# Linear attention with a GELU feed-forward: weights in another row order, and the masks of batch 1 on GpSimd

## The chip, the cores and the metric

One core of one Trainium2 chip. The metric is device time in microseconds (us) of one execution, median over several. The page of a profile covers a slightly shorter span (292.0 us for an execution that took 293.77 us). A "look" is one profiled execution, and there is one per kernel.

## The reference

For 8 batches, 8 heads, 576 tokens and 64 dimensions per head, linear attention and then a feed-forward layer:

```python
def phi(x):
    return np.where(x > 0, x, np.exp(x) - 1.0) + 1.0
q_p, k_p = phi(q), phi(k)
kv = np.einsum('bhsd,bhse->bhde', k_p, v)          # per head 64 x 64
z = np.sum(k_p, axis=2)
num = np.einsum('bhsd,bhde->bhse', q_p, kv)
den = np.einsum('bhsd,bhd->bhs', q_p, z)[..., None] + 1e-06
x = num / den                                       # tokens x 512 after the heads are joined
h = x @ w_in                                        # 512 -> 2048
g = gelu_tanh(h)
out = g @ w_out                                     # 2048 -> 512
```

## The kernel before

TensorE does everything in bf16. Each batch is one stage `j` of the feed-forward layer, with a first half (16 blocks `m` of 128 hidden units, `h_ps`) and a second half (16 slots of four 128x512 matmuls, `o_ps`). The attention of the next batch is placed by hand into slots of these halves. The first 512 tokens of a batch ("main") and the last 64 ("rests") are loaded and handled apart.

The parts that the change touches:

```python
w_in_r = moe_w_in.rearrange("(c p) f -> p c f", p=P)
w_out_r = moe_w_out.rearrange("(i p m) f -> i p m f", p=P, m=4)   # 8-KB runs: 4 rows per partition
# ...
def cast_w_in_halves(i):              # f32 -> bf16 on GpSimd, every fourth column
    for u in range(2):
        nc.gpsimd.tensor_copy(
            out=w_in_sb[:, :, 512 * i + 256 * u : 512 * i + 256 * (u + 1)]
                .rearrange("p c (m x) -> p c m x", m=2),
            in_=w_st[i].rearrange("p c (x m) -> p c m x", m=4)[:, :, 2 * u : 2 * u + 2],
        )

def mask_vrh(b, pairs):               # v's rests times 0 or 1 per partition: keep one pair of heads
    for i in pairs:
        nc.scalar.activation(vrh[b][:, :, i, 0:D], rest_by_head("vr", b), AF.Copy,
                             scale=pair[:, i : i + 1])
# ...
def plan_second():                    # batch 1, inside stage 0
    def exps():                       # ScalarE, after the GELU of block 11
        # ... exp of q (two halves), of k, of k's rests, then the GELU table again
    def phis():                       # VectorE: max(x+1, 1), then the minimum with exp
        for s in halves:
            phi_line(phi["q", b], ld["q", b], s)
            phi_min(phi["q", b], box["q"], s)
        phi["k", b] = phi_of(ld["k", b], box["k"], "k_p")
        phi_krh(1)                    # the rests of k
        mask_vrh(1, range(NP))
    # ...
    at(1, 0, 11, exps)
    at(2, 0, 0, phis)
    at(2, 0, 0, cast_vs)
    for fn, c, slot in (
        (tq, 0, 8), (tq, 1, 8),                  # q transposed, into 2 PSUM buffers
        (lambda c: kv_rests(), 0, 9),            # rests' matmuls, on krh and vrh
        (lambda c: kv(), 0, 10),                 # main sum of k*v
        (lambda c: last_w_out(), 0, 10),
        (nab, 0, 11), (nab, 1, 12),              # q times kv
        # ...
    ):
        at(2, 0, slot, lambda fn=fn, c=c: fn(c))
```

PSUM is the memory into which TensorE writes its results. The two PSUM buffers that `tq`, `kv_rests`, `kv` and `nab` share in turn are also those of blocks 12 to 15 of stage 0, which ScalarE's GELUs have to empty first. Each engine works in program order. GpSimd has, in this order, eight casts of `w_in`, six of `w_out` and a seventh; ScalarE does the eighth.

Of the kernel before, what the change touches and what calls it, by code (L numbers as in the profile page):

```python
# [10 lines left out]
AF = mybir.ActivationFunctionType  # L11
ALU = mybir.AluOpType
# [3 lines left out]
def kernel(  # L16
# [12 lines left out]
    nc = tc.nc  # L29

    B, H, S, D = q.shape
    d_model, d_ff = moe_w_in.shape
    P = 128
# [21 lines left out]
    small = ctx.enter_context(tc.tile_pool(name="small", bufs=1))  # L55

    w_in_r = moe_w_in.rearrange("(c p) f -> p c f", p=P)
    w_out_r = moe_w_out.rearrange("(i p m) f -> i p m f", p=P, m=4)

    w_in_sb = const.tile([P, KM, d_ff], BF16, name="w_in_sb")  # L60
    w_out_sb = const.tile([P, MM, d_model], BF16, name="w_out_sb")
# [15 lines left out]
    def load_rest_half(src, t, m, s, eng):  # L77
        eng.dma_start(
            out=t[REST * s : REST * (s + 1)],
            in_=src[2 * m + s, :, MAIN:S, :].rearrange("h p d -> p h d"),  # L80
        )
# [7 lines left out]
    def load_w_in(i, t=None, f=slice(0, 512)):  # L89
        if t is None:  # L90
            t = pld.tile([P, KM, 512], FP32, name="w_st", tag="ld")
        nc.sync.dma_start(
            out=t[:, :, f], in_=w_in_r[:, :, 512 * i + f.start : 512 * i + f.stop]
        )
        return t

    def load_w_out(i):
        t = pld.tile([P, 4, 512], FP32, name="w_st", tag="ld")
        nc.sync.dma_start(out=t, in_=w_out_r[i])
        return t  # L100

    ld = {}
# [7 lines left out]
    def load_rests(m, names):  # L110
        for n, src in names:
            ld[n, m] = load_rest(src, m, n[0] + "_r", nc.gpsimd)
# [16 lines left out]
    def rest_by_head(n, b):  # L129
        return ld[n, 0][:, C * b : C * b + C]  # L130
# [5 lines left out]
    w_st = [load_w_in(i) for i in range(3)]  # L136
# [14 lines left out]
    pair = small.tile([P, NP], FP32, name="pair")  # L151
# [10 lines left out]
    vrh, krh = [], []  # L162
# [13 lines left out]
    for b in range(2):  # L176
        nc.gpsimd.tensor_copy(
            out=vrh[b][:, :, :, D], in_=pair[:, None, :].to_broadcast([P, C, NP])
# [10 lines left out]
    def gelu_table():  # L189
        nc.scalar.preload_act_table_set("gelu_apprx_tanh_and_others")  # L190

    def cast_w_in_halves(i):
        for u in range(2):

            nc.gpsimd.tensor_copy(  # L195
                out=w_in_sb[
                    :, :, 512 * i + 256 * u : 512 * i + 256 * (u + 1)
                ].rearrange("p c (m x) -> p c m x", m=2),
                in_=w_st[i].rearrange("p c (x m) -> p c m x", m=4)[
                    :, :, 2 * u : 2 * u + 2  # L200
                ],
            )

    def cast_w_out_halves(i, fns):
        for u, fn in enumerate(fns):
            fn(
                out=w_out_sb[:, 4 * i + 2 * u : 4 * i + 2 * u + 2, :],
                in_=wo_st[i][:, 2 * u : 2 * u + 2, :],
            )


    phi = {}
# [4 lines left out]
    def exp_into(e, x, hs=slice(0, H)):  # L217
        nc.scalar.activation(  # L218
            e[:, :, hs, :].rearrange("p c h d -> p h c d"), by_chunk(x[:, hs]), AF.Exp
        )  # L220

    def exp_main(name, b):
        e = pe.tile([P, C, H, D], BF16, name=name + "_e")
        exp_into(e, ld[name, b])
        return e


    def phi_line(xp, x, hs=slice(0, H)):
        nc.vector.tensor_scalar(  # L229
            xp[:, :, hs, :].rearrange("p c h d -> p h c d"), by_chunk(x[:, hs]),  # L230
            1.0, 1.0, op0=ALU.add, op1=ALU.max,
        )

    def phi_min(xp, e, hs=slice(0, H)):
        nc.vector.tensor_tensor(  # L235
            xp[:, :, hs, :], xp[:, :, hs, :], e[:, :, hs, :], op=ALU.min
        )

    def phi_of(x, e, name):
        xp = pphi.tile([P, x.shape[2] // D, H, D], BF16, name=name)  # L240
        phi_line(xp, x)
        phi_min(xp, e)
        return xp
# [7 lines left out]
    def cast_v(b, fn, s=slice(0, H)):  # L251
        fn(
            out=vps[b % 2][:, s, :, 0:D],
            in_=ld["v", b][:, s].rearrange("p h (c d) -> p h c d", d=D),
        )
# [5 lines left out]

    def mask_vrh(b, pairs):
        for i in pairs:
            nc.scalar.activation(
                vrh[b][:, :, i, 0:D], rest_by_head("vr", b), AF.Copy,
                scale=pair[:, i : i + 1],
            )

    def exp_krh(b):
        nc.scalar.activation(krh[b][0][:, :, 0], rest_by_head("kr", b), AF.Exp)  # L270

    def phi_krh(b):

        e, line, kr = krh[b]
        nc.vector.tensor_scalar(
            line[:, :, 0], rest_by_head("kr", b), 1.0, 1.0, op0=ALU.add, op1=ALU.max
        )
        nc.vector.tensor_tensor(line[:, :, 0], line[:, :, 0], e[:, :, 0], op=ALU.min)
        for t in range(2):
            nc.vector.tensor_scalar(  # L280
                kr[:, :, t], line[:, :, 0], odd[:, t : t + 1], None, op0=ALU.mult
            )
# [52 lines left out]
    def t_q(src_of, qt, c0, n, t_ps):  # L335
        for c in range(n):
            for i in range(NP):
                nc.tensor.transpose(  # L338
                    t_ps[:, c, i, :], src_of(c0 + c, i), ident
                )  # L340
# [197 lines left out]
    def at(ph, j, slot, fn):  # L538
        fill.setdefault((ph, j, slot), []).append(fn)
# [92 lines left out]
    def plan_second():  # L632

        b = 1
        box = {}

        def exps():
            box["q"] = pe.tile([P, C, H, D], BF16, name="q_e")
            for s in halves:
                exp_into(box["q"], ld["q", b], s)  # L640
            box["k"] = exp_main("k", b)
            exp_krh(1)
            gelu_table()

        def phis():
            phi["q", b] = pphi.tile([P, C, H, D], BF16, name="q_p")
            for s in halves:
                phi_line(phi["q", b], ld["q", b], s)
                phi_min(phi["q", b], box["q"], s)
            phi["k", b] = phi_of(ld["k", b], box["k"], "k_p")  # L650
            phi_krh(1)
            mask_vrh(1, range(NP))

        def cast_vs():
            cast_v(b, nc.vector.tensor_copy)

        def last_w_out():
            cast_w_out_halves(3, (nc.gpsimd.tensor_copy, nc.scalar.copy))
            load_rests(1, (("kr", k), ("vr", v)))
            for s in range(2):  # L660
                load_rest_half(q, ld["qr", 0], 0, s, nc.gpsimd)
            load_rests(1, (("qr", q),))

        def kv():
            kv_ps = ps_a.tile([P, 2, 512], FP32, name="kv_ps", tag="a")
            for i in range(NP):
                kv_mm(b, i, kv_ps)
            kv_evac(b, kv_ps, second=box["rests"])

        def kv_rests():  # L670
            r_ps = ps_a.tile([P, 2, 512], FP32, name="r_ps", tag="a")
            for a in range(2):
                kv_mm_rests(b, a, r_ps[:, a, 0 : 2 * E])
            box["rests"] = pout.tile([P, 2, d_model], FP32, name="o_sb")[
                :, :, 0 : 2 * E
            ].rearrange("p a (t u) -> p a t u", u=E)
            nc.scalar.copy(
                box["rests"],
                r_ps[:, :, 0 : 2 * E].rearrange("p a (t u) -> p a t u", u=E),
            )  # L680

        def tq(h):
            if h == 0:
                box["qt"] = pt.tile([P, C, NP, P], BF16, name="qt")
            t_ps = ps_a.tile([P, 4, NP, P], BF16, name="t_ps", tag="a")
            t_q(q_src(b), None, 2 * h, 2, t_ps)
            nc.scalar.copy(out=box["qt"][:, 2 * h : 2 * h + 2], in_=t_ps[:, 0:2])

        def nab(c):
            n_ps = ps_a.tile([P, 2, 512], FP32, name="n_ps", tag="a")  # L690
            nab_mm(box["qt"][:, c], kvbds[b], n_ps)
            box["x", c] = nab_evac(n_ps)

        def tx(c):
            copy = nc.scalar.copy if c < 2 else nc.vector.tensor_copy
            pe_tx(b, c, box["x", c], c < 2, copy)

        def early(m):
            first_mm_early(1, m)

        at(1, 0, 11, exps)
        at(2, 0, 0, phis)
        at(2, 0, 0, cast_vs)
        for fn, c, slot in (
            (tq, 0, 8), (tq, 1, 8), (lambda c: kv_rests(), 0, 9), (lambda c: kv(), 0, 10), (lambda c: last_w_out(), 0, 10),
            (nab, 0, 11), (nab, 1, 12), (nab, 2, 13), (tx, 0, 13), (nab, 3, 14),
            (tx, 1, 14), (tx, 2, 15), (early, 0, 15), (early, 1, 15), (tx, 3, 15),
            (early, 2, 15),
        ):
            at(2, 0, slot, lambda fn=fn, c=c: fn(c))  # L710
# [209 lines left out]
```

## Time and profile before

| | before |
|---|---|
| time, median | 293.55 us (293.38 to 293.57) |
| span of the profile | 292.0 us |
| TensorE busy | 283.3 us, 97% |
| second half of stage 0 begins | 33.64 us |
| first product of q with batch 1's sum (`n_ps`) | 46.65 us |

The last two rows are the marks by which kernels are compared: from the first `n_ps` on, TensorE is fed without a gap that the change touches, so a shift there is a shift of the end. Here is, from the timeline of TensorE, the stretch in which batch 1's attention starts (start, duration of the group, instruction, shapes, number; in brackets idle time before and what ended it):

```profile
41.41 1.06 PE L338 MATMUL t_ps<-ident,q_p 128*128 128x128 bf16 x16
...
43.17 0.62 PE L287 MATMUL r_ps<-g 128*128 128x130 bf16 x8
...
44.49 1.10 PE L301 MATMUL kv_ps<-vp,k_p 128*128 128x130 bf16 x16
...
46.65 0.41 PE L344 MATMUL n_ps<-kvbd,qt 128*128 128x130 bf16 x4 [0.20 <-DVE kvbd L328]
```

Transposes, rests, sum and product run without a wait but the last 0.20 us. In the trace the mask tiles bear the name `g`, since they lie in the buffer of a later `g`.

### The profile page before, as it was taken

What the parts mean: (1) busy time and instruction counts of PE and PEld (TensorE: products, weight loads), DVE (VectorE), ACT (ScalarE), POOL (GpSimd) and SP (SyncE); (2) the same over time, 40 slices, a digit from 0 to 9 for tenths busy, and PEclk for the clock granted to TensorE, in tenths of its full rate; (3) what the DMA queues carried; (4) which work ended last, traced back from release to release, by engine and by line L of the source; (5) the groups of instructions that cost most, each with busy time, mean ns of one, the idle gap of its engine ahead of it and who ended that gap; (6) DMA issues with size and microseconds to landing.
All of it is one profiled execution on the core that took longest, in us unless ns stands there. A gap on an engine that the chain in (4) does not pass through costs nothing.

```text
span 292.0 us, 4298 instructions
## 1 busy us (share of the span) xinstructions
PE 283.3 (97%) x1710; PEld 147.6 (51%) x1710; DVE 115.7 (40%) x191; ACT 161.2 (55%) x228; POOL 45.8 (16%) x57
## 2 busy tenths in 40 slices
PE   8789999999999999999999999999999999999994
PEld 7665455645565445544454445444544444444443
DVE  4950495606683692347035642452240000000011
ACT  4847894589955753666356925672551166026400
POOL 7089968300007000000000000000000000000000
PEclk9999999999999999999999999999999999999999
DMA  7999999993379994999922993305140110020032
GB/s 249 378 409 410 362 399 361 325 382 93 72 246 220 287 242 144 290 257 292 332 53 65 288 277 110 72 2 162 54 74 18 72 74 0 31 94 21 0 72 72
DMA packets 62835, 53.75 MB, mean 184 GB/s; under 512 B 31840, under 2 KB 57184, under 8 KB 62304
## 3 DMA queue, kind: packets, MB, share of 16 engines
q1 hardware_dynamic: 59392, 42.35, 51.7%
q10 hardware_dynamic: 2464, 8.52, 7.3%
q0 software_dynamic: 960, 2.62, 3.2%
q8 instruction: 13, 0.21, 0.3%
q14 instruction: 6, 0.05, 0.1%
HBM read 36.70 MB, written 9.44 MB: 158 GB/s over the span
## 4 chain that ended last, share of the span: by engine, by line
PE 87%; POOL 6%; DMA 3%; SPq 1%; DVE 1%; issue 0%; DVEq 0%
PE o_ps L843 41%; PE h_ps L392 39%; POOL w_in_sb L195 6%; DMA w_st<-in_moe_w_in_dram 3%; PE n_ps L344 3%; PE kv_ps L301 2%; PE o_ps L812 1%; SPq L69 1%; PE kv_ps L312 0%; SPq L124 0%; PE t_ps L367 0%; PE t_ps L338 0%; DVE kvbd L328 0%; PE r_ps L287 0%; DVE xt L488 0%
## 5 line engine op out<-in xcount | busy, mean ns | idle before, releaser
L843 PE MATMUL o_ps<-w_out_sb,g 128*128 128x512 bf16 x560 | 124.4, 379 | 0.0
L392 PE MATMUL h_ps<-xt,w_in_sb 128*128 128x512 bf16 (+2 forms) x588 | 119.7, 351 | 1.0 <-POOL w_in_sb L195 0.9
L800 ACT ACTIVATE g<-h_ps 128x512 bf16<-128x512 f32 x144 | 84.2, 598 | 50.5 <-PE h_ps L392 49.6
L392 PEld LDWEIGHTS <-w_in_sb 128*128 128x128 bf16 x652 | 58.9, 98 | 55.1 <-POOL w_in_sb L195 2.0
L843 PEld LDWEIGHTS <-g 128*128 128x128 bf16 x560 | 54.1, 98 | 62.9
L858 ACT COPY o_sb<-o_ps 128x512 f32<-128x512 f32 x18 | 10.6, 587 | 59.5 <-PE o_ps L843 59.5
L856 DVE COPY o_sb<-o_ps 128x512 f32<-128x512 f32 x17 | 11.7, 688 | 66.3 <-PE o_ps L843 66.3
L356 DVE TENSOR_TENSOR x<-n_ps,r 128x512 bf16<-128x512 f32 x36 | 24.9, 691 | 1.2
L333 DVE CAST kvbd<-kv_ps 64x260 bf16<-64x260 f32 (+1 forms) x14 | 5.7, 407 | 35.0 <-PE kv_ps L312 34.7
L195 POOL CAST w_in_sb<-w_st 128x1024 bf16<-128x1024 f32 x8 | 16.2, 2090 | 8.0 <-DMA w_st<-in_moe_w_in_dram 8.0
L218 ACT ACTIVATE k_e<-k_x 128x2048 bf16<-128x2048 f32 (+1 forms) x9 | 15.5, 1719 | 3.4 <-DMA k_x<-in_k_dram 3.3
L354 DVE RECIPROCAL r<-n_ps 128x8 f32<-128x8 f32 x36 | 7.4, 206 | 24.7 <-PE n_ps L344 24.7
L235 DVE TENSOR_TENSOR q_p<-q_p,q_e 128x2048 bf16<-128x2048 bf16 (+1 forms) x10 | 11.3, 1131 | 14.4 <-ACT q_e L218 13.6
L218 ACT ACTIVATE q_e<-q_x 128x2048 bf16<-128x2048 f32 (+1 forms) x10 | 15.5, 1557 | 0.8 <-DMA q_x<-in_q_dram 0.8
L235 DVE TENSOR_TENSOR k_p<-k_p,k_e 128x2048 bf16<-128x2048 bf16 (+1 forms) x9 | 10.6, 1178 | 11.9 <-ACT k_e L218 11.4
L392 PE MATMUL h_ps<-xt_rest,w_in_sb 128*128 128x512 bf16 x64 | 14.0, 379 | 0.0
L344 PEld LDWEIGHTS <-qt 128*128 128x128 bf16 x128 | 9.8, 98 | 7.5 <-DVE kvbd L328 0.7
L229 DVE TENSOR_SCALAR q_p<-q_x 128x2048 bf16<-128x2048 f32 (+1 forms) x10 | 10.9, 1093 | 6.0 <-DMA q_x<-in_q_dram 5.9
L344 PE MATMUL n_ps<-kvbd,qt 128*128 128x130 bf16 x128 | 12.7, 221 | 0.4 <-DVE kvbd L328 0.2
L229 DVE TENSOR_SCALAR k_p<-k_x 128x2048 bf16<-128x2048 f32 (+1 forms) x9 | 11.5, 1275 | 2.6 <-DMA k_x<-in_k_dram 2.6
L301 PEld LDWEIGHTS <-k_p 128*128 128x128 bf16 x128 | 9.3, 96 | 5.3 <-issue 0.3
L301 PE MATMUL kv_ps<-vp,k_p 128*128 128x130 bf16 x128 | 11.4, 220 | 0.0
(64 smaller groups left out, 141.7 us busy)
## 6 DMA issues: line engine op xcount, KB each, us to landing
out_dram<-o_sb ACTq DMA_DIRECT2D x16, 512.0 KB, 3.7
k_x<-in_k_dram SPq DMA_DIRECT2D x7, 1024.0 KB, 9.6
v_x<-in_v_dram SPq DMA_DIRECT2D x7, 1024.0 KB, 11.6
q_x<-in_q_dram SPq DMA_DIRECT2D x6, 1024.0 KB, 8.5
w_st<-in_moe_w_in_dram SPq DMA_DIRECT2D x4, 1024.0 KB, 12.0
w_st<-in_moe_w_out_dram SPq DMA_DIRECT2D x4, 1024.0 KB, 10.2
q_x<-in_q_dram SPq DMA_DIRECT2D x4, 512.0 KB, 9.3
k_x<-in_k_dram SPq DMA_DIRECT2D x2, 512.0 KB, 4.2
```

The costliest lines, as they stand in the source:

```text
L195: nc.gpsimd.tensor_copy(out=w_in_sb[:, :, 512 * i + 256 * u : 512 * i + 256 * (u + 1)].rearrange("p c (m x) -> p c m x", m=2), in_=w_st[i] ...
L218: nc.scalar.activation(e[:, :, hs, :].rearrange("p c h d -> p h c d"), by_chunk(x[:, hs]), AF.Exp)
L229: nc.vector.tensor_scalar(xp[:, :, hs, :].rearrange("p c h d -> p h c d"), by_chunk(x[:, hs]), 1.0, 1.0, op0=ALU.add, op1=ALU.max,)
L235: nc.vector.tensor_tensor(xp[:, :, hs, :], xp[:, :, hs, :], e[:, :, hs, :], op=ALU.min)
L301: nc.tensor.matmul(dst, lhsT=kp[:, c, P * i : P * (i + 1)], rhs=vps[b % 2][:, 2 * i : 2 * i + 2, c, :], start=(c == 0 and b > 0), stop=(c ...
L344: nc.tensor.matmul(n_ps[rows, i // 2, 2 * E * (i % 2) : 2 * E * (i % 2) + 2 * E], lhsT=qt_c[:, i, rows], rhs=kvbd[:, i, :], skip_group_che ...
L356: nc.vector.tensor_tensor(x, n_v[:, :, :, 0:D], r[:, :, :, None].to_broadcast([P, 2, 4, D]), op=ALU.mult,)
L392: nc.tensor.matmul(h_ps[:, tok], lhsT=w_in_sb[:, c, P * m : P * (m + 1)], rhs=xt[:, c, tok], start=(c == 0), stop=(c == KM - 1), skip_grou ...
L800: nc.scalar.activation(gs[j][:, i, :], ps, AF.Gelu_apprx_tanh)
L843: nc.tensor.matmul(o_pss[t], lhsT=g[:, m, P * t : P * (t + 1)], rhs=w_out_sb[:, m, :], start=(m == 0), stop=(m == MM - 1),)
L856: nc.vector.tensor_copy(dst, o_ps)
L858: nc.scalar.copy(dst, o_ps)
```

## The change

Its intent: the casts of `w_in` read every fourth float, because `w_out` is loaded with four neighbouring rows per partition and the hidden units have to correspond. If `w_out` is loaded in runs of one row (2 KB), `w_in` needs no permutation, and its cast reads without a stride. The first half then ends sooner, so batch 1's preparation is adjusted: masks off ScalarE, rests' maps first, q transposed a slot sooner, the rests' matmuls a slot later.

```diff
-    w_out_r = moe_w_out.rearrange("(i p m) f -> i p m f", p=P, m=4)
+    w_out_r = moe_w_out.rearrange("(m p) f -> p m f", p=P)
@@ load_w_out
-        nc.sync.dma_start(out=t, in_=w_out_r[i])
+        nc.sync.dma_start(out=t, in_=w_out_r[:, 4 * i : 4 * i + 4, :])
@@ cast_w_in_halves
             nc.gpsimd.tensor_copy(
-                out=w_in_sb[
-                    :, :, 512 * i + 256 * u : 512 * i + 256 * (u + 1)
-                ].rearrange("p c (m x) -> p c m x", m=2),
-                in_=w_st[i].rearrange("p c (x m) -> p c m x", m=4)[
-                    :, :, 2 * u : 2 * u + 2
-                ],
+                out=w_in_sb[:, :, 512 * i + 256 * u : 512 * i + 256 * (u + 1)],
+                in_=w_st[i][:, :, 256 * u : 256 * (u + 1)],
             )
@@ mask_vrh
-            nc.scalar.activation(
-                vrh[b][:, :, i, 0:D], rest_by_head("vr", b), AF.Copy,
-                scale=pair[:, i : i + 1],
-            )
+            out_i, src = vrh[b][:, :, i, 0:D], rest_by_head("vr", b)
+            if b == 0:
+                nc.scalar.activation(out_i, src, AF.Copy, scale=pair[:, i : i + 1])
+            else:
+                nc.gpsimd.tensor_scalar(
+                    out_i, src, pair[:, i : i + 1], None, op0=ALU.mult
+                )
@@ phis
-            phi["k", b] = phi_of(ld["k", b], box["k"], "k_p")
             phi_krh(1)
             mask_vrh(1, range(NP))
+            phi["k", b] = phi_of(ld["k", b], box["k"], "k_p")
@@ slots
-            (tq, 0, 8), (tq, 1, 8), (lambda c: kv_rests(), 0, 9), (lambda c: kv(), 0, 10), ...
+            (tq, 0, 7), (tq, 1, 7), (lambda c: kv_rests(), 0, 10), (lambda c: kv(), 0, 10), ...
```

More of the change, by code (lines that the diff above doesn't have):

```diff
@@ L704, in plan_second @@
         for fn, c, slot in (
-            (tq, 0, 8), (tq, 1, 8), (lambda c: kv_rests(), 0, 9), (lambda c: kv(), 0, 10), (lambda c: last_w_out(), 0, 10),
+            (tq, 0, 7), (tq, 1, 7), (lambda c: kv_rests(), 0, 10), (lambda c: kv(), 0, 10), (lambda c: last_w_out(), 0, 10),
             (nab, 0, 11), (nab, 1, 12), (nab, 2, 13), (tx, 0, 13), (nab, 3, 14),
```

## The prediction

> **What bounds the kernel now.** The page's first two parts come first: is one engine full, and where is it not?
>
> ```profile
> PE 283.3 (97%) x1710; PEld 147.6 (51%) x1710; DVE 115.7 (40%) x191; ACT 161.2 (55%) x228; POOL 45.8 (16%) x57
> PE   8789999999999999999999999999999999999994
> POOL 7089968300007000000000000000000000000000
> DMA  7999999993379994999922993305140110020032
> ```
>
> TensorE is busy 97% of a 292.0 us span. Its slices of 7.3 us fall under 9 only in the first three, that is before 22 us, and in the last. The change touches nothing after 66 us, so all it can win is idle TensorE time, some 9 us in all, and only the share in its stretch. The chain that ended last says which part that is. Columns: start, duration, what.
>
> ```profile
> 5.43 10.14 DMA w_st<-in_moe_w_in_dram
> 15.57 0.05 issue
> 15.62 16.24 POOL w_in_sb L195 x8
> 31.86 0.04 issue
> 31.91 1.90 PE h_ps L392 x8
> 33.81 7.77 PE o_ps L843 x36
> ```
>
> From 15.62 to 31.86 the chain runs through the eight GpSimd casts of w_in. Before them it waits for the first w_in load, which the change leaves alone; after 53.49 it is TensorE and nothing else until 288.1. But a chain through GpSimd for 16.24 us isn't 16.24 us lost: TensorE works beside it. The timeline of TensorE shows what it lost:
>
> ```profile
> 18.37 0.39 PE L367 MATMUL t_ps<-ident,x 128*128 128x128 bf16 x4
> 19.65 1.07 PE L392 MATMUL h_ps<-xt,w_in_sb 128*128 128x128 bf16 x16 [0.90 <-POOL w_in_sb L195]
> 20.56 0.39 PE L367 MATMUL t_ps<-ident,x 128*128 128x128 bf16 x4
> 20.78 13.03 PE L392 MATMUL h_ps<-xt,w_in_sb 128*128 128x128 bf16 x88
> ```
>
> Transposes of the size of the first line take 0.22 us to the next start (17.69 less 17.45 earlier in that timeline), so TensorE was free at about 18.6 and began at 19.65, when the second cast had ended: 1.05 us (0.90 by the modelled ends). Then it is nearly continuous. The second loss lies before the last pair of slices (m = 14, 15), which waits for cast eight: from 20.78 the work is 40 matmuls of 128 columns at 0.057 us (0.23 for four) and 40 of 512 columns at 0.216 us (0.86 for four), 2.3 + 8.6, hence 31.7; the chain has it start at 31.91. That is 0.2 us. The weight-load timeline agrees: idle 0.55 us for POOL there.
>
> **What one cast costs.** The GpSimd timeline, first casts of w_in and then of w_out:
>
> ```profile
> 15.62 2.02 POOL L195 CAST w_in_sb<-w_st 128x1024 bf16<-128x1024 f32 x1 [8.02 <-DMA w_st<-in_moe_w_in_dram]
> 17.58 2.02 POOL L195 CAST w_in_sb<-w_st 128x1024 bf16<-128x1024 f32 x1
> 31.79 1.05 POOL L206 CAST w_out_sb<-w_st 128x1024 bf16<-128x1024 f32 x1
> 33.75 1.51 POOL L206 CAST w_out_sb<-w_st 128x1024 bf16<-128x1024 f32 x1
> 34.28 1.52 DVE L229 TENSOR_SCALAR q_p<-q_x 128x1024 bf16<-128x1024 f32 x1
> ```
>
> Same engine, same size and types. The w_in cast reads every fourth float (16 bytes apart) and takes 2.02 us; the w_out cast reads without a stride and takes 1.05 us. Beside VectorE work from SBUF it takes 1.5 to 2.0 us, and VectorE pays as well: this 128x1024 line takes 1.52 us here, against 0.70 us at 27.31.
>
> **The Trainium skill.** "GPSIMD Engine Reference", Performance pitfalls for Q7 kernels, says that reads with step times element size above 8 bytes cost some 2.9 instead of 1.9 cycles per element. The trace agrees in direction and shows more: 1.97 against 1.03 ns per element, a factor of 1.9. The same page, Specifications, says that GpSimd's SBUF interfaces are shared with VectorE, with contention in a two-port mode or with two SBUF inputs; the pairs 1.05/1.51 and 0.70/1.52 us agree. Its section Engine selection calls one-input GpSimd operations roughly line-rate; no masked GpSimd copy is in this trace, so I scale from the cast. "DMA: Bandwidth & Descriptors", Specifications, puts the minimum transfer for line rate at 512 bytes; w_out's new 2-KB runs are above it. The trace can't separate them from 8-KB ones, but from 12 to 24 us, where w_in's 2-KB runs are in flight, it moved 400 to 429 GB/s.
>
> **Part by part.**
> 1. *w_in cast without the stride.* Eight casts from 2.02 to about 1.05 us; next to VectorE's work on PSUM at 16 to 20 us the old casts weren't slowed, so I take 1.0 us from start to start. Casts 1 and 2 end at about 16.7 and 17.7. After that loads pace them: at 408 GB/s a MB takes 2.6 us, so loads two to four land near 18.2, 20.8 and 23.4 (an estimate), and the last cast ends near 25.5, not 31.86. TensorE, free at 18.6, no longer waits: transposes (0.22), 64 small matmuls less the 8 already done (3.2) and 48 large ones (10.4) end the stage at 32.4 instead of 33.64: **1.05 + 0.2 = 1.25 us won**. GpSimd's saving of 8 us is off the path beyond that.
> 2. *w_out in 2-KB runs.* The same bytes; needed so that the hidden units of both weights correspond. w_out's casts still follow their loads. The third load's casts began at 37.76; its rows m = 8, 9 are needed at slot 8, which I put at 40.4. Hidden: 0. The fourth is cast from 42.8 on and needed near 45.8. Hidden too.
> 3. *Masks of v from ScalarE to GpSimd.* Off ScalarE: four at 0.43, 1.73 us at 39.88. On GpSimd: four of 256 elements, estimated 0.4 to 0.5 us each from 1.05 us for 1024 plus a fixed part (a 16-element cast there takes 0.2), 1.6 to 2.0 us. In GpSimd's order they stand after the casts of w_out's third load, 41.25 in the kernel before, so they end at about 43.0. The matmuls of the rests are now at slot 10. From 32.4: eight slots of 0.86 to 39.3, q's transposes 0.89, three slots 2.6, 43.1 with the wait of part 5. So they come just in time; I charge 0.1 us.
> 4. *Rests' maps ahead of k's.* VectorE does the same work in another order. v's cast ended at 43.45 before and was needed at 44.65. q's maps can start 1 us sooner, so v's cast ends near 42 and is needed near 43.6. Hidden: 0.
> 5. *q transposed at slot 7.* TensorE reaches it at 39.3. Its PSUM buffers are those of m = 12 to 15, released by the GELUs that ended at 40.0. These follow the exponentials of k, which began at 34.42 when k landed (wait 0.39), so loads pin them, not TensorE. The second half of the transposes would be at 39.75 and waits to 40.0: **0.25 to 0.3 us lost**. Without masks on ScalarE, q's copies follow at once.
>
> Sum: -1.25 + 0.3 + 0.1 = -0.85 us, or -1.25 if the loads run a little earlier. The chain behind (v's sum, VectorE's add of 0.87 us, next product) keeps its 0.2 us wait and only moves. From 293.55 I get 292.3 to 292.7, and say **292.5 us**.
>
> **Rivals.**
> - *The load stream takes the place of the casts.* The DMA row is 9 from slice 1 to 8, so earlier releases of w_in's buffers only lengthen the queue: k of batch 1 still lands at 34.4. If it governed the second half, nearly everything would be given back, 293.3 us. Against it: behind k only the 0.3 us of part 5 is short, and v and w_out's last quarter have 1 us or more.
> - *GpSimd becomes the bound in batch 1.* Four masks beside VectorE's maps could take 0.8 us each (a cast went from 1.05 to 2.03 there), ending past 44.4: 1.2 us of stall, and w_out's last cast late too, 293.5 to 294. For it: GpSimd stands ahead of the sums in order. Against it: VectorE has little to do from 42 to 44.6.
> - *The gain is larger.* If 8-KB runs were the slower ones (370 GB/s at 24 to 26 us, 353 at 32 to 36), k lands up to 1 us sooner, the waits of parts 3 and 5 vanish and the second half may tighten: 292.0.
> - *All 16 us of the chain.* Someone who reads the chain's shares might halve GpSimd's 16.24 us and expect 285. TensorE was busy for all but 1.25 us of it.
>
> **Range and chances.** 2% is 5.9 us; all of TensorE's idle time is 8.7 us, most of it before the first w_in load lands or at the end. So faster by over 2%: 1%. Slower by over 2% would need a stall of over 7 us: 1%. Within 2%: 98%. The range runs from all of the gain with 0.4 us on top (291.8) to hardly any gain (293.4).
>
> **What would show it right or wrong.** Right: casts of w_in at about 1.05 us and then idle for loads; TensorE's 0.90 us wait gone; its second half beginning near 32.4; a wait of about 0.3 us at q's transposes; the first stage of batch 1's GELUs starting about 1 us sooner than 54.12; everything later shifted by the same amount. Wrong: casts still near 1.5 us or over (the stride wasn't the cost), a new wait of TensorE for GpSimd at the rests' matmuls, for a w_out cast, or for v; or a load landing 1 us late because of 2-KB runs.

## The result, and the profile after

The changed kernel takes **297.36 us** (median of 4, 296.32 to 297.64) against 293.56 us (293.38 to 293.67) of the kernel before, with one execution more than in the table above. The ratio is 1.0124, interval 1.0099 to 1.0149. (A ratio is the mean time of one kernel's fast runs over the mean of the other's in the same rounds, so not quite the ratio of the medians.) It is slower by 1.2%, inside the 2% band, and well outside the range predicted. Three executions took 297.25 to 297.64 us at a mean granted clock of 0.994, and one 296.32 us at 1.000. That difference returns below. Executions over 1.5% slower than the fastest of the same kernel are left out of the means.

The page, the lines that answer to those of before, and the row of the granted TensorE clock:

```profile
PE 285.9 (97%) x1710; PEld 149.5 (51%) x1710; DVE 115.4 (39%) x191; ACT 159.5 (54%) x224; POOL 43.5 (15%) x61
PE   8999977999999999999999999999999999999994
...
PEclk9999997999999999999999999999999999999999
```

TensorE's slices 1 and 2, once 7 and 8, are now 9; slices 5 and 6 (37 to 52 us) fell to 7, and the clock dips in slice 6. The gain came, and a larger loss came after it. The chain that ended last (start, duration, what) names it:

```profile
29.12 8.94 DMA w_st<-in_moe_w_out_dram
...
38.11 3.80 POOL w_out_sb L201 x2
41.90 4.61 POOL g L263 x4
...
46.55 0.59 PE r_ps L285 x4
47.15 1.73 PE kv_ps L299 x16
48.88 1.47 PE o_ps L841 x4
```

The eight casts of `w_in` no longer carry the chain. In GpSimd's timeline they come in pairs, each pair in some 2.03 us after a wait for its load, for example:

```profile
18.32 2.03 POOL L194 CAST w_in_sb<-w_st 128x1024 bf16<-128x1024 f32 x2 [0.99 <-DMA w_st<-in_moe_w_in_dram]
```

The chain now runs through the third load of `w_out`, its two casts and the four GpSimd masks, 4.61 us. TensorE's timeline shows the waits:

```profile
17.99 1.06 PE L390 MATMUL h_ps<-xt,w_in_sb 128*128 128x128 bf16 x16
...
31.70 7.07 PE L841 MATMUL o_ps<-w_out_sb,g 128*128 128x512 bf16 x32
39.50 0.61 PE L336 MATMUL t_ps<-ident,q_p 128*128 128x128 bf16 x8 [0.72 <-ACT g L798]
40.48 0.61 PE L336 MATMUL t_ps<-ident,q_p 128*128 128x128 bf16 x8 [0.37 <-ACT g L798]
40.92 2.75 PE L841 MATMUL o_ps<-w_out_sb,g 128*128 128x512 bf16 x12
44.74 0.39 PE L285 MATMUL r_ps<-g 128*128 128x130 bf16 x4 [1.07 <-POOL g L263]
46.55 0.59 PE L285 MATMUL r_ps<-g 128*128 128x130 bf16 x4 [1.43 <-POOL g L263]
46.94 1.94 PE L299 MATMUL kv_ps<-vp,k_p 128*128 128x130 bf16 x16
...
50.19 0.40 PE L342 MATMUL n_ps<-kvbd,qt 128*128 128x130 bf16 x4
```

The 0.90 us wait for the second cast is gone, and the second half begins at 31.70. Then come two waits for GELUs, two for the masks, and after them matmuls at half speed (`kv_ps` 1.94 us instead of 1.10 for the same 16). Counted by starts, with 0.216 us per 512-column matmul, 0.45 us for eight transposes and 0.23 us for four rests' matmuls:

| what moved the first `n_ps` (46.65 before, 50.19 after) | us |
|---|---|
| second half begins at 31.70, not 33.64 | -1.94 |
| q's transposes: 39.50 instead of 38.61, and 0.53 between them | +1.42 |
| rests' matmuls: 44.74 instead of 43.51, and 1.58 between them | +2.81 |
| half clock: sum 0.95 to 1.73, slot 11 0.86 to 1.47 | +1.39 |
| wait for VectorE's add, hidden by the slow slot | -0.19 |
| sum (measured: +3.54) | +3.49 |

The span grew by 3.5 us too, so what comes after adds nothing. What a mask costs is in GpSimd's timeline:

```profile
41.89 1.88 POOL L263 TENSOR_SCALAR g<-v_r,pair 128x256 bf16<-128x256 f32 x1
43.77 0.92 POOL L263 TENSOR_SCALAR g<-v_r,pair 128x256 bf16<-128x256 f32 x1
```

A mask takes 0.92 us by itself, and 1.88 us next to VectorE's cast of v, which itself takes 2.06 us instead of 1.22. The times look like taking turns rather than like both running slower: of the mask's 1.88 us (from 41.89), 1.09 us lie before the end of VectorE's cast (40.92 to 42.98) and 0.79 us after it. No run here tests that. On ScalarE one took 0.43 us from start to start.

### The profile page after: what moved, and what is told of

It reads as the page before. It is cut to its first block, busy times and chain, and to the rows that moved or that the text cites. A ratio compares the mean times of both kernels' runs of the same rounds, so it can differ in the third digit from the quotient of the medians.

```text
span 295.5 us, 4299 instructions
## 1 busy us (share of the span) xinstructions
PE 285.9 (97%) x1710; PEld 149.5 (51%) x1710; DVE 115.4 (39%) x191; ACT 159.5 (54%) x224; POOL 43.5 (15%) x61
## 4 chain that ended last, share of the span: by engine, by line
PE 83%; DMA 7%; SPq 5%; POOL 4%; issue 0%; DVE 0%; DVEq 0%
PE o_ps L841 38%; PE h_ps L390 37%; DMA w_st<-in_moe_w_in_dram 4%; DMA w_st<-in_moe_w_out_dram 3%; PE n_ps L342 3%; PE kv_ps L299 3%; SPq L124 2%; POOL g L263 2%; POOL w_out_sb L201 1%; SPq L69 1%; PE o_ps L810 1%; SPq L92 1%; POOL w_in_sb L194 1%; PE kv_ps L310 0%; PE t_ps L365 0%
## 5 line engine op out<-in xcount | busy, mean ns | idle before, releaser
L224 DVE TENSOR_SCALAR q_p<-q_x 128x2048 bf16<-128x2048 f32 (+1 forms) x10 | 11.6, 1155 | 8.0 <-DMA q_x<-in_q_dram 7.9
L299 PEld LDWEIGHTS <-k_p 128*128 128x128 bf16 x128 | 10.1, 103 | 5.1 <-issue 0.3
L299 PE MATMUL kv_ps<-vp,k_p 128*128 128x130 bf16 x128 | 12.2, 231 | 0.0
L414 PE MATMUL w_ps<-warm 128*128 128x252 bf16 x74 | 11.0, 313 | 1.0 <-DVE warm L141 1.0
L224 DVE TENSOR_SCALAR k_p<-k_x 128x2048 bf16<-128x2048 f32 (+1 forms) x9 | 10.3, 1148 | 2.7 <-DMA k_x<-in_k_dram 2.7
```

What stands on the lines that cost most here:

```text
L224: nc.vector.tensor_scalar(xp[:, :, hs, :].rearrange("p c h d -> p h c d"), by_chunk(x[:, hs]), 1.0, 1.0, op0=ALU.add, op1=ALU.max,)
L299: nc.tensor.matmul(dst, lhsT=kp[:, c, P * i : P * (i + 1)], rhs=vps[b % 2][:, 2 * i : 2 * i + 2, c, :], start=(c == 0 and b > 0), stop=(c ...
L414: nc.tensor.matmul(w_ps[:, 0:252], lhsT=warm[:, 0:P], rhs=warm)
```

## The experiments

Theory: the masks on GpSimd are dear, stand behind load-paced casts, and the idle time brings the half clock. Rivals: the load stream (k and `w_out`'s third quarter) is what rules, whatever is done with the masks; 2-KB runs slow that stream; or the clock drops for a reason of its own.

**Masks back on ScalarE, all else as changed.**

```diff
-            if b == 0: ... else: nc.gpsimd.tensor_scalar(out_i, src, pair[:, i : i + 1], None, op0=ALU.mult)
+            nc.scalar.activation(out_i, src, AF.Copy, scale=pair[:, i : i + 1])
```

> The changed kernel with batch 1's four masks of v back on ScalarE, all else as changed. Mask theory (the GpSimd masks, 0.92 us each alone and 1.88 us beside VectorE, hold up the rests' matmuls by 2.5 us, and the idle stretch brings a half clock on top): the two waits of TensorE for GpSimd at 42 to 47 us are gone, no slice at half clock, and the time falls to 292.5 to 293.3 us, below the kernel before. Load theory (k and w_out's third quarter landing 0.3 to 0.4 us later, and the waits behind them, are the loss): the time stays above 295 us.

Measured: 293.56 us (293.07 to 293.88), ratio to before 0.9991 (0.9978 to 1.0004): the same. No half clock (0.997 to 1.000 in all five). So the masks' place on GpSimd, with what follows from it, is the whole loss of 1.2%. But the gain that I had expected below the kernel before didn't come. TensorE's timeline:

```profile
31.58 7.07 PE L838 MATMUL o_ps<-w_out_sb,g 128*128 128x512 bf16 x32
39.84 0.61 PE L333 MATMUL t_ps<-ident,q_p 128*128 128x128 bf16 x8 [1.19 <-ACT g L795]
40.82 0.61 PE L333 MATMUL t_ps<-ident,q_p 128*128 128x128 bf16 x8 [0.37 <-ACT g L795]
```

By starts, q's transposes lose 1.35 + 0.53 us here. So the waits behind the loads have a part in the missing gain (the last runs below narrow it), though none in the loss.

**The GpSimd masks alone, on the kernel before** (only `mask_vrh` of the diff).

> The kernel before with only the four masks of batch 1 moved to GpSimd; the rests' matmuls still at slot 9. Mask theory: the masks begin after the cast at 41.25, take about 4.5 us, and the rests' matmuls end near 46 instead of 43.8; with some idle time hidden nowhere, 295.8 us without a clock drop and about 297 us with one. Load theory: no change, 293.5 us.

Measured: 296.75 us (296.04 to 298.00), ratio 1.0108 (1.0081 to 1.0135). TensorE waits 1.14 and 1.42 us for the masks. Two executions at a mean clock of 0.998 took 296.04 and 296.08 us, two at 0.994 took 297.42 and 298.00; in the profiled one, of the latter kind, the half clock comes after the waits. The part alone does the damage; neither the weights nor the order are needed for it.

**The weights alone, on the kernel before** (`w_out_r`, `load_w_out` and `cast_w_in_halves` of the diff).

> The kernel before with the two weight edits alone (cast of w_in without a stride, w_out in 2-KB runs); masks on ScalarE, old order, q transposed at slot 8. If the weight edits are all gain: second half of stage 0 begins 1.3 to 1.9 us sooner than before's 33.64, then about 1 us is given back where q's transposes or w_out's third quarter wait for loads; 292.3 to 293.0 us. If 2-KB runs hurt the load stream, the time is 293.6 us or more.

Measured: 293.62 us (293.41 to 294.12), ratio 0.9998 (0.9985 to 1.0010): no change. I had expected most of the gain to survive, and was wrong. The number falls on the branch in which 2-KB runs hurt the loads; the next two runs test that.

**2-KB runs of `w_out` alone** (wrong result: the rows don't match).

> The kernel before with w_out in 2-KB runs alone; its rows then don't match the permuted w_in, so the result is wrong on purpose. If 2-KB runs are as fast as 8-KB ones: k of batch 1 lands at 34.4 as before and the time is 293.5 us. If they slow the loads: k lands 0.3 to 0.8 us later, as it did in the three kernels with 2-KB runs, and the time is up to 0.5 us longer.

Measured: 293.63 us (293.42 to 294.04), ratio 1.0010 (0.9996 to 1.0024). Its first GpSimd cast starts at 15.28 us, like the run above (15.32, on another chip), so the two make a pair with and without the stride. TensorE with the strided casts, then with the contiguous ones:

```profile
33.33 7.93 PE L843 MATMUL o_ps<-w_out_sb,g 128*128 128x512 bf16 x36
...
46.33 0.41 PE L344 MATMUL n_ps<-kvbd,qt 128*128 128x130 bf16 x4 [0.20 <-DVE kvbd L328]
```

```profile
31.68 7.07 PE L838 MATMUL o_ps<-w_out_sb,g 128*128 128x512 bf16 x32
39.06 1.02 PE L838 MATMUL o_ps<-w_out_sb,g 128*128 128x512 bf16 x4 [0.31 <-POOL w_out_sb L201]
...
42.86 0.61 PE L282 MATMUL r_ps<-g 128*128 128x130 bf16 x8 [1.01 <-ACT qt L682]
...
46.33 0.41 PE L339 MATMUL n_ps<-kvbd,qt 128*128 128x130 bf16 x4 [0.20 <-DVE kvbd L323]
```

The second half begins 1.65 us sooner, and the first `n_ps` comes at the same 46.33: all of it is given back, 0.47 us waiting for the third quarter of `w_out` (its load landed at 37.9) and 1.18 us for ScalarE, whose chain hangs on k's load (exponential of k, table, GELUs, masks, copies of q).

**Contiguous casts with `w_out` still in 8-KB runs** (wrong result).

> The kernel before with the contiguous cast of w_in alone, w_out still in 8-KB runs; the rows don't match, so the result is wrong on purpose. It goes beside the run with both weight edits (293.62 us). If 2-KB runs cost 0.3 to 0.6 us in the landing of k: k's exponential starts near 34.0 here, and the time is 293.0 to 293.3 us. If they cost nothing: k at 34.7 and 293.6 us.

Measured: 293.39 us (293.28 to 293.50), ratio 0.9996 (0.9984 to 1.0009), next to 0.9998 for the version with 2-KB runs. The two ran on different chips, each beside the kernel before. k's exponential, where it waits for the load, began at 34.56 here, at 34.42 in the kernel before and at 35.12 with the GpSimd masks alone, all three with 8-KB runs, and at 34.68 to 35.18 in the versions with 2-KB runs. The two ranges overlap, so no delay through 2-KB runs is seen, in the landings or in the times. One of a few tenths isn't excluded (the interval of 2-KB runs alone reaches to 1.0024, 0.7 us).

**Dummy matmuls in the two waits of the changed kernel.**

```diff
             for a in range(2):
+                for _ in range((12, 13)[a]):
+                    nc.tensor.matmul(r_ps[:, a, 260:512], lhsT=warm[:, 0:P], rhs=warm)
                 kv_mm_rests(b, a, r_ps[:, a, 0 : 2 * E])
```

> The changed kernel with 12 and 13 dummy matmuls of 252 columns put into TensorE's two waits for the masks (their results are overwritten or never read). If the half clock from 46.5 to 50 us follows from the idle stretch before it: full clock there and 1.0 to 1.5 us less than the changed kernel in its half-clock executions, some 296.0 to 296.4 us in all executions. If the clock drop has another cause: the half clock stays and the time is as the changed kernel's, 297.3 us.

Measured: 296.24 us (296.05 to 296.27), clock 0.997 to 1.000 in all five. The table by stretches (TensorE, weight loads, VectorE, ScalarE, GpSimd, then granted clock, DMA share, GB/s) has, for the changed kernel and then for this one:

```profile
46.00:48.00 2.00, 1.45 (x14) 1.44 (x14) 0.00 (x0) 0.82 (x2) 2.00 (x3) 0.64 1.09 386
48.00:50.00 2.00, 2.00 (x13) 1.16 (x11) 0.85 (x2) 0.50 (x1) 2.00 (x4) 0.51 1.09 386
```

```profile
46.00:47.00 1.00, 1.00 (x16) 0.84 (x14) 0.00 (x0) 0.17 (x1) 1.00 (x2) 1.00 1.09 360
```

More work, and 1.1 us less time than the changed kernel's median. So the half clock follows from the idle stretch before it. It costs 0.9 to 1.3 us, and the changed kernel's one execution without it (296.32) falls on the time of this run.

**Masks on GpSimd, ahead of the third quarter's casts.**

```diff
-    for i in range(3):
+    for i in range(2):
         cast_w_out_halves(i, (nc.gpsimd.tensor_copy,) * 2)
@@ phis
             mask_vrh(1, range(NP))
+            cast_w_out_halves(2, (nc.gpsimd.tensor_copy,) * 2)
```

> The changed kernel with the GpSimd masks put ahead of the casts of w_out's third quarter in GpSimd's order, so that they run in its idle time from 34.5 to 38 us. If the place in the order is what hurts: masks at 36 to 40.5 us, no TensorE wait for them, but the casts end 1 to 2 us later and TensorE waits for them at slot 8; 294 to 295 us, and no half clock. If the cost per mask alone matters wherever it stands: 296.5 us or more.

Measured: 297.63 us (296.42 to 299.12), ratio 1.0147 (1.0116 to 1.0177). The masks ran from 35.85 to 41.4, and TensorE waited for the casts behind them instead (1.31 us) and, against my expectation, was at half clock again after it: the granted clock was 0.50 from 43 to 46 us, and 12 matmuls took 4.44 us instead of 2.75. The cost of the masks hurts in both of the places tried; this one isn't the better place that I expected.

**What in a mask is dear?** Two variants of the changed kernel: plain casts of the same shape, and a multiplication by a constant. Their outputs are wrong, which doesn't matter for the times.

```diff
-                nc.gpsimd.tensor_scalar(out_i, src, pair[:, i : i + 1], None, op0=ALU.mult)
+                nc.gpsimd.tensor_copy(out_i, src)                                   # first
+                nc.gpsimd.tensor_scalar(out_i, src, 1.0, None, op0=ALU.mult)        # second
```

> The changed kernel with the GpSimd masks replaced by plain GpSimd casts of the same shape, so that nothing is masked and the result is wrong on purpose. If the scalar multiply is what is dear on GpSimd: each takes 0.3 to 0.5 us (0.27 by the w_out cast's rate and a fixed part) instead of 0.92 to 1.88, the masks end near 43.7, and the time is 293.5 to 294.3 us. If the shape (four runs of 64 elements) is dear: 0.9 us each as before and 296 to 297.5 us.

> The changed kernel with the GpSimd masks multiplying by the constant 1.0 instead of a value per partition; the result is wrong on purpose. If the per-partition operand is dear: each takes 0.40 us alone, as the plain cast of that shape did. If the scalar operation itself is dear on GpSimd: 0.92 us alone as in the changed kernel.

Measured: with casts 294.11 us (293.87 to 294.48), ratio 1.0026; with the constant 296.79 us (a single execution, state unknown, half clock in it). One cast of that shape in GpSimd's timeline, and the constant multiplications (shortest/median/longest in ns):

```profile
43.49 0.40 POOL L263 CAST g<-v_r 128x256 bf16<-128x256 f32 x1
```

```profile
L263 POOL TENSOR_SCALAR g<-v_r x4: 837/846/1811, 41.9 to 45.3; 128x256 bf16<-128x256 f32 x4
```

0.40, 0.85 and 0.92 us: the scalar operation itself is dear on GpSimd, not the shape and hardly the value per partition. A cast was what I had scaled from.

**Where the gain could come out.** Three versions with the masks on ScalarE. First, ScalarE's exponentials of batch 1 go after the last GELU of stage 0, so that no PSUM buffer waits for k's load:

```diff
-        at(1, 0, 11, exps)
+        at(1, 0, 15, exps)
```

> The changed kernel with the masks on ScalarE, and ScalarE's exponentials of batch 1 after the last GELU of stage 0 instead of after the twelfth. PSUM theory (q's transposes wait 1.1 to 1.6 us because the GELUs that free their PSUM buffers stand behind k's exponential, which waits for k's load): those GELUs end near 32, the transposes wait for nothing, about 1.3 us less than with the masks on ScalarE alone, 292.0 to 292.6 us. If the load stream rules the second half in any order: w_out's third quarter or k's sum waits instead, 293.2 us or more.

Measured: 293.51 us (293.19 to 293.57), ratio 1.0002 (0.9988 to 1.0015). The expected gain didn't come. The transposes wait for nothing, but 0.50 us by starts are now lost at `w_out`'s third quarter, and the rest one step on, in front of the sum:

```profile
44.23 1.11 PE L296 MATMUL kv_ps<-vp,k_p 128*128 128x130 bf16 x16 [1.27 <-DVE vp L247]
```

Second, VectorE's order on top of it, with both of q's lines in its idle time and the rests after k:

```diff
             for s in halves:
                 phi_line(phi["q", b], ld["q", b], s)
+            for s in halves:
                 phi_min(phi["q", b], box["q"], s)
-            phi_krh(1)
             mask_vrh(1, range(NP))
             phi["k", b] = phi_of(ld["k", b], box["k"], "k_p")
+            phi_krh(1)
```

> The run with ScalarE's exponentials last, and VectorE's work for batch 1 in another order: both q lines first, in the time in which it waits for the exponentials, then q's minima, k, the rests, v. In that run v's sum waited 1.27 us for v's cast on VectorE, which was the last of its queue. If VectorE's order is what kept the gain from coming out: v's cast ends near 41.5 instead of 44.2, v's sum begins near 43.0 (then held by the copies of q on ScalarE), and the time is 292.2 to 292.6 us. If something else stands right behind it, w_out's last quarter or the load of v: 293 us or more.

Measured: **292.62 us** (292.47 to 293.11), ratio **0.9972** (0.9959 to 0.9986). It beats the kernel before by 0.3%. v's cast ended at 43.25, not at 41.5 as expected, and which of the two moves on VectorE helped wasn't separated. What is left in front of the sum:

```profile
43.31 1.11 PE L296 MATMUL kv_ps<-vp,k_p 128*128 128x130 bf16 x16 [0.51 <-ACT o_sb L673]
```

Third, the GELU table's load (1.28 us on ScalarE) moved behind q's copies (dropped from `exps`, placed at slot 11):

> The run above, with the load of the GELU table (1.28 us on ScalarE) moved from before the masks and q's copies to slot 11, after them. If the copies held v's sum: 0.1 to 0.3 us less than the run above, 292.0 to 292.4 us. If not, the same time.

Measured: 292.68 us (292.49 to 293.12), ratio 0.9972 (0.9960 to 0.9985): no more. The 0.51 us wait is now put down to v's cast on VectorE. Of 1.65 us won in the first half, 0.8 to 0.9 us reaches the end.

## Why the prediction was wrong

It said 292.5 us, with 291.8 to 293.4; 297.36 us was measured. By its steps:

1. *Casts without the stride: right.* They take 1.0 us from start to start, are paced by loads, and TensorE's second half begins 1.94 us sooner, or 1.65 us in the pair with the same first landing. Predicted: 1.25 us. Of the 1.94 us, some 0.6 us is not the change's: batch 0's last transposes before the wait began at 17.77 instead of 18.37, and at 17.81 in a version with the old casts.
2. *2-KB runs hidden: right*, within what the runs can tell (1.0010, 0.9996 to 1.0024).
3. *Masks on GpSimd: this term of the sum failed.* It read "estimated 0.4 to 0.5 us each from 1.05 us for 1024 plus a fixed part", and charged 0.1 us. A cast of that shape does take 0.40 us, but the mask isn't a cast: 0.92 us alone, 1.88 us beside VectorE. The four end at 46.5, not 43.0 (0.64 us of that because they start at 41.89, not 41.25), and by starts TensorE loses 2.81 us. The second rival had the wait, and nearly the size of a mask (0.8 us), but from contention with VectorE, and was put down because VectorE has little to do from 42 us; three of the four masks took 0.92 us without contention. Masks alone on the kernel before: 1.0108.
4. *The half clock: not in the prediction at all.* The waits together left TensorE nearly idle for 3 us, and the 3.4 us after that ran at half clock, +1.39 us. Filled waits: 296.24 us at full clock.
5. *q's transposes: right mechanism, wrong size.* 0.25 to 0.3 us was predicted, 1.42 us measured, since TensorE came 0.7 us sooner than reckoned and k's load 0.4 us later, which lies in the spread of its landings.
6. *Rests' maps first: right, hidden.* v's cast ended at 43.0, well before the sum, and with the masks on ScalarE the kernels with and without the new order take 293.56 and 293.62 us.

Two things that I set against each other were both true. The waits behind the loads took back all of the casts' gain (the first rival; the weights alone give 0.9998), and the masks came on top. It wasn't the loads by themselves: with the same loads and another order of the work, 0.8 to 0.9 us of it came out. Even with masks at 0.4 us the time would have been 293.6 to 294.1, as the runs with masks on ScalarE and with plain casts show, so the sum had two errors, not one. What stays open: why k's load lands anywhere from 34.4 to 35.2 us. The length of the runs doesn't explain it: in the three versions with 8-KB runs it was 34.42, 34.56 and 35.12, one look each.

Three readings of the prediction were off without consequence: 17.69 less 17.45 is 0.24, not 0.22; the 16-element cast took 0.26 us on average, not 0.2; and all of the gain with 0.4 us on top gives 291.9, not 291.8.

## What to carry to other kernels

Before an operation is moved to an idle engine, its cost there has to come from that operation on that engine: a cast's rate doesn't price a scalar multiplication. When a paced stage becomes faster, look at what its consumers wait for next; here the queues behind it hung on the same loads, and part of the gain only came out when work that doesn't need the late load was put ahead of work that does. A wait on TensorE can cost more than its length: here two waits of 2.8 us together brought another 0.9 to 1.3 us at half clock in most executions.

## What the Trainium skill lacked or had wrong

- "GPSIMD Engine Reference", Performance pitfalls for Q7 kernels: reads stepping more than 8 bytes are given as 2.9 instead of 1.9 cycles per element, half as much again. Here the stride of 16 bytes took a 128x1024 cast from 1.05 to 2.02 us, almost twice.
- "GPSIMD Engine Reference", Engine selection: one-input operations are called roughly line-rate. That fits the cast (1.05 us for 128x1024, 0.40 us for 128x256), but the one-input scalar multiplication took 0.85 us with a constant and 0.92 us with a value per partition. The page has no figure for it.
- "TensorE: Matmul & The Clock Gate", Part 1, the table of the two states: half rate after at least one idle window of some 3.4 us. The rate (0.50) and its length (46.56 to 50.0 us, 3.4 us) agree. But the stretch before it was shorter (2.9 us) and not wholly idle: 1.2 and 1.6 us of waiting with four matmuls between them were enough in three of four executions of the changed kernel, and not in the fourth.
